# Loads, mask, strided row order and normalisation of the first attention batch

## The chip, the core and the metric

One core of one Trainium2 chip runs the whole program. The metric is device time in microseconds of one execution; the kernel before took 893.43 us (median of 3 runs, 892.42 to 893.95).

## What is computed

Sparse attention, then two MLPs. q, k and v have shape (4 batches, 8 heads, 576 positions, 64).

- Heads 0 to 3 (local): a query sees itself and the 31 positions before it.
- Heads 4 to 7 (strided): a query sees earlier positions with the same remainder modulo 32, itself included; that is 18 positions (j) for each of the 32 residues (r).
- Scores are scaled by 1/8, masked, put through a softmax (sum plus 1e-9) and multiplied by v.
- The result x, 2304 tokens by 512, goes through (x Wa * x Wb) Wo with inner width 1536, then through silu(x Win) Wout2 with inner width 2048. The weights come as float64.

```
scores = where(mask, q @ k.T / 8, -1e9);  attn = softmax(scores);  x = attn @ v
y = ((x @ w_a) * (x @ w_b)) @ w_out
h = y @ w_in2;  out = (h * sigmoid(h)) @ w_out2
```

## The kernel before, in words

**Words.** The float64 weights are cut into pieces of 128 x 512 values. Each arrives as 32-bit words, 512 KB in one of five buffers ("words"), and is converted to float32 on the core. The first six pieces (0 to 5) go a short way: step 0 on GpSimd (L739), step 1 on VectorE (L747), a rebase on ScalarE (L701, tile e), step 2 on VectorE (L752). A buffer is free when its words have been read by these. Then split_w (L774, L775) makes two fp32r halves, with which TensorE multiplies in three passes. Pieces 0 to 4 are a0, b0, a1, b1 (columns of Wa, Wb) and o0 (rows of Wo). Later pieces are converted by sign_w, merge_w and rebase_w inside the blocks, some blocks ahead, and are stored for later token groups.

**First batch.** Attention of batch 0 runs before any block, as a pipeline over nine units: 0 to 4 are local (windows of 128 queries, the last of 64), 5 to 8 are strided (the groups of residues of RES). The loop at L937 runs stages s = -1, 0, 1, ..., and in each stage emits the steps of ORDER = "AXPV0QWS1LGRTBKUON2Y". Each engine works in the order in which its instructions are emitted. For stage s:

- S: scores of unit s on TensorE. Only in the first batch the mask is put into PSUM by a product with the identity (L459), in front of the products (L466).
- L, G: maxima of unit s (L488), and 1e-9 added to the sums of unit s-1 (guard, L523), both VectorE.
- X: exponentials of unit s-1, ScalarE (L500).
- N: reciprocal on VectorE (L527) and product on GpSimd (L538) for unit s-1.
- T, U: transposes (L558) and copies (L567, L572) for unit s-3. V, O: products with v (L607) and stores (L636 ScalarE, L639 VectorE) for unit s-5.
- R: prepare; for strided units GpSimd scales the queries into qs, one instruction for each residue group (L427). PREP puts units 5 and 6 into stage 3, unit 7 into 5, unit 8 into 7.
- Q: transposes of the strided tables on VectorE (L325). P: the local tables.
- 0, 1, B, 2, Y: conversion of piece CONV[s] and split of the one of the stage before. A: half of a first product of blocks 0 to 3 (PART; L782 into acc). K: idle products that keep TensorE warm (L885).
- W: loads that LOADS gives to stage s.

LOADS[-2] is issued before the loop. A capital letter puts the load on ScalarE's queue, the others go on SP's, which issues in order. q, k: local tables; t: strided q, k (qld, kld); m: masks; s: strided v (vs, 16 transfers of 45 or 13.5 KB); w: words; u: next batch's q, k; b: cast of the strided mask. Local v (vl) goes on GpSimd's queue.

**Row order of strided units.** Constant mask rows come as (j, r). The kernel keeps query rows as (r, j), so the mask is loaded in six transfers that permute its rows (L910), and cast into mask_str by GpSimd at stage 3. The columns of the products with v are written through a "p r j" view of PSUM, which makes them (j, r) again for the store.

**Afterwards** come blocks, one for each product with a piece for a token group of 512. Batches 1 to 3 are spread over the blocks by plan_attention: batch 1 transposes its q, k in blocks 0 and 1, and its normalisation, too, is on GpSimd. Within a block, words of the piece eight blocks on are loaded.

Of the kernel before, what the change touches and what calls it, by code (L numbers as in the profile page):

```python
# [9 lines left out]
F32 = mybir.dt.float32  # L10
F32R = mybir.dt.float32r
BF16 = mybir.dt.bfloat16
# [5 lines left out]
ALU = mybir.AluOpType  # L18
AX = mybir.AxisListType

P = 128
STRIDE = 32
HALF = 64
TAKE = 3

RES = [(0, 3, 6), (9, 12, 15), (18, 21, 24), (27, 29)]
# [14 lines left out]
LOADS = {  # L41
    -2: (
        "q0 Q1 i M1 k0 K1 K2 Q2 t8 m7 s2 w0 s2 s1 w2 s2 s1 w1 s1 s1 s1 w4 "
        "w3 s5 u2 u5 u2"
    ),
    3: "b",
    8: "w5 w6",
    10: "w7",
    11: "w11",
    12: "w8 w9",  # L50
    16: "w10",
}
# [8 lines left out]

CONV = {5: 0, 8: 1, 10: 2, 11: 3, 13: 4, 14: 5}
PART = {11: 0, 12: 1, 15: 2, 16: 3}
# [65 lines left out]
def attention_gated_mlp_silu_mlp(  # L129
# [15 lines left out]
    nc = tc.nc  # L145
# [41 lines left out]
    ident_b = cpool.tile([P, P], BF16, name="ident_b")  # L187
    lead.tile([P, 32], F32, name="lead")
    mask_loc = apool.tile([P, 4, HALF], BF16, name="mask_loc", bufs=1)
# [82 lines left out]
    class Batch:  # L272
# [125 lines left out]
        def prepare(self, u):  # L398
# [20 lines left out]
            else:  # L419
                res = RES[i]  # L420
                ng = len(res)
                st = dict(w=JR, segs=2 * ng, slots=ng, n=J * (res[-1] - res[0] + TAKE))
                st["mask"] = mask_str.unsqueeze(1).to_broadcast([P, 2 * ng, JR])
                qh = queries[i % 2]
                if self.first:
                    for g, r0 in enumerate(res):
                        nc.gpsimd.tensor_scalar_mul(  # L427
                            qh[:, :, g, :JR].rearrange("p c (r j) -> p c r j", r=TAKE),
                            qT.rearrange("p c (j r) -> p c r j", r=STRIDE)[:, :, r0:r0 + TAKE],
                            SCALE,  # L430
                        )
# [97 lines left out]
        def normalise(self, u):  # L529
            ty, i = self.units[u]  # L530
            st = self.state[u]
            segs, w, ng = st["segs"], st["w"], st["slots"]
            rs = st["rs"]
            if self.first:
                self.invert(u)
            pr, rs = st["pr"][:, :ng, :, :w], rs.rearrange("p (i g) -> p g i", i=2)
            rs = rs.unsqueeze(3).to_broadcast([P, ng, 2, w])
            nc.gpsimd.tensor_tensor(out=pr, in0=pr, in1=rs, op=ALU.mult)  # L538

# [34 lines left out]
        def values(self, *us):  # L574
# [6 lines left out]
            for u in us:  # L581
                i, st = self.units[u][1], self.state[u]
                pt = st["pt"]
                for g in range(st["slots"]):
                    for k in range(2 if ty == 0 else 1):
                        for hp in range(2):
                            for c in range(2):
# [8 lines left out]
                                else:  # L596
                                    r0 = RES[i][g]
                                    keys = slice(HALF * hp, HALF * hp + JR)
                                    out = banks[hp][rows, :first["cols"]].rearrange("p (j r) -> p r j", j=J)
                                    parts.append((  # L600
                                        out[:, r0 - RES[self.units[us[0]][1]][0]:][:, :TAKE],
                                        vs[keys, firsts.index(r0), c, :],
# [273 lines left out]
    with tc.manual_schedule():  # L876
# [17 lines left out]
        masks[0] = masks[0].rearrange("p (s k) -> p s k", k=HALF)  # L894
        nc.gpsimd.memset(masks[1], 0.0)

        def startup_loads(names):

            for name in names.split():
# [5 lines left out]
                elif name[0] == "m" and n == 1:  # L905
                    feed[0].dma_start(out=masks[0], in_=mask_loc_d)
                elif name[0] == "m":
                    for h in range(0, P, HALF):
                        for r in range(TAKE):
                            feed[0].dma_start(  # L910
                                out=masks[1][h + J * r:h + J * (r + 1)],
                                in_=mask_str_d[h:h + JR].rearrange("(j r) k -> r j k", r=TAKE)[r],
                            )
                elif name[0] == "b":
                    nc.gpsimd.tensor_copy(out=mask_str, in_=masks[1])
                elif name[0] in "qk":
# [580 lines left out]
        p = 0  # L1497
# [130 lines left out]
```

## Time and profile before

| what | value |
|---|---|
| median of 3 runs | 893.43 us (892.42 to 893.95) |
| profiled execution | 891.74 us |
| its span, first to last instruction | 890.0 us |
| mean granted TensorE clock | 0.996 |
| TensorE busy | 876.0 us (98%) |
| VectorE busy | 633.4 us (71%) |
| ScalarE busy | 542.7 us (61%) |
| GpSimd busy | 162.2 us (18%) |
| HBM | 149 GB/s over the span |

The profile is of one execution. Engines: PE is TensorE, PEld its weight loads, DVE VectorE, ACT ScalarE, POOL GpSimd, SP SyncE; SPq is SP's queue issuing transfers. L538 is line 538. Shares over the whole span average a start, in which a chain through all engines decides, with a long rest in which TensorE is hardly ever idle.

### The profile page before, as it was taken

Reading aid. Unit: us, or ns where it says so; the run is one execution under the profiler, and the core shown is the slowest. Engines: PE = TensorE matmul, PEld = TensorE weight load, DVE = VectorE, ACT = ScalarE, POOL = GpSimd, SP = SyncE. Lnnn points to the kernel's source line nnn. Section 1 sums busy time; section 2 is a strip of 40 time slices with the busy share of each in tenths; the row PEclk is TensorE's granted clock in tenths of the full one; section 3 lists DMA queues with packets and bytes.
Section 4 is the critical chain, followed back from the end, with each engine's and each line's share of the span. In section 5 each row is a group of like instructions: output and inputs, shape, how many; then the busy total and the mean of one; then the engine's idle time right before and its main releaser. Section 6 shows DMA issues by size and latency. Waiting matters only on the chain.

```text
span 890.0 us, 16103 instructions
## 1 busy us (share of the span) xinstructions
PE 876.0 (98%) x5859; PEld 728.6 (82%) x5866; DVE 633.4 (71%) x1175; ACT 542.7 (61%) x1296; POOL 162.2 (18%) x232
## 2 busy tenths in 40 slices
PE   8799999999999999999999999999999999999998
PEld 5578788888887788899888888888888888898987
DVE  4687877767667665888776768776777697766664
ACT  4779898676786756675444344755554565455553
POOL 5664564444433110100000000000000000000000
PEclk9899999999999999999999999999999999999999
DMA  9999999798999922664122122321121242311201
GB/s 185 220 252 294 281 282 295 228 288 266 311 301 269 304 82 95 190 190 143 47 72 62 57 71 71 115 75 59 60 72 53 93 162 71 132 59 51 80 1 71
DMA packets 152977, 133.77 MB, mean 150 GB/s; under 512 B 91522, under 2 KB 114690, under 8 KB 152898
## 3 DMA queue, kind: packets, MB, share of 16 engines
q1 hardware_dynamic: 143986, 108.59, 43.4%
q0 software_dynamic: 7424, 23.34, 7.2%
q8 instruction: 46, 0.75, 0.3%
q10 hardware_dynamic: 1488, 0.82, 0.3%
q14 instruction: 33, 0.27, 0.1%
HBM read 110.16 MB, written 22.54 MB: 149 GB/s over the span
## 4 chain that ended last, share of the span: by engine, by line
PE 86%; DVE 5%; ACT 4%; DMA 2%; issue 1%; POOL 1%; SPq 1%; POOLq 0%; ACTq 0%; DVEq 0%
PE ring L782 17%; PE acc L1167 13%; PE ring L1103 12%; PE att L1103 9%; PE ring L1167 7%; PE att L1167 7%; PE acc L1103 7%; PE acc L1538 6%; PE acc L1566 3%; PE att L607 1%; ACT prs L500 1%; PE acc L885 1%; PE att L466 1%; DMA vs<-in_v_dram 1%; DVE w L775 1%
## 5 line engine op out<-in xcount | busy, mean ns | idle before, releaser
L1432 DVE TENSOR_TENSOR w<-raw,w 128x512 fp32r<-128x512 f32 (+1 forms) x164 | 103.2, 641 | 14.8 <-ACT w L1431 14.1
L782 PE MATMUL ring<-x1a,w 128*128 128x256 f32 (+1 forms) x480 | 99.0, 327 | 0.0
L1431 ACT CAST w<-raw 128x512 fp32r<-128x512 f32 (+1 forms) x164 | 93.1, 581 | 7.3 <-ACT w L1431 3.0
L1103 PE MATMUL ring<-L,w 128*128 128x512 f32 x360 | 87.8, 389 | 0.0
L1216 POOL DMA_DIRECT2D out_dram<-o x12 | 6.5, 543 | 407.8 <-DVE o L1215 398.9
L1103 PEld LDWEIGHTS ring<-L,w 128*128 128x128 f32 x360 | 67.6, 188 | 14.0
L1167 PE MATMUL acc<-w,h 128*128 128x512 f32 x288 | 78.5, 391 | 0.0
L782 PEld LDWEIGHTS ring<-x1a,w 128*128 128x128 f32 x480 | 71.5, 190 | 7.7
L775 DVE TENSOR_TENSOR w<-raw,w 128x512 fp32r<-128x512 f32 x80 | 61.6, 777 | 14.2 <-ACT w L774 14.1
L1538 PE MATMUL acc<-h,w 128*128 128x512 f32 x288 | 70.5, 394 | 0.6 <-ACT h L792 0.4
L792 ACT CAST h<-h 128x512 fp32r<-128x512 f32 (+1 forms) x48 | 27.2, 567 | 71.9 <-DVE h L1140 40.5
L1538 PEld LDWEIGHTS acc<-h,w 128*128 128x128 f32 x288 | 53.2, 188 | 12.4 <-ACT h L792 0.6
L1167 PEld LDWEIGHTS acc<-w,h 128*128 128x128 f32 x288 | 53.6, 188 | 9.4 <-DVE h L793 0.4
L727 POOL TENSOR_SCALAR raw<-words 128x512 f16<-128x512 uint8 x56 | 51.8, 926 | 42.5 <-DMA words<-in_moe_w_out_dram 9.8
L782 PE MATMUL ring<-x,w 128*128 128x512 f32 x240 | 58.2, 394 | 0.3 <-DVE w L775 0.3
L1167 PE MATMUL acc<-h,w 128*128 128x256 f32 (+1 forms) x288 | 53.5, 336 | 0.0
L782 PEld LDWEIGHTS ring<-x,w 128*128 128x128 f32 x240 | 44.3, 188 | 10.6 <-DVE w L775 1.6
L1167 PE MATMUL ring<-w,h 128*128 128x512 f32 x192 | 51.9, 391 | 0.0
L774 ACT CAST w<-raw 128x512 fp32r<-128x512 f32 x80 | 49.2, 623 | 1.3 <-DMA raw<-keptp 1.3
L1167 PEld LDWEIGHTS acc<-h,w 128*128 128x128 f32 x288 | 45.2, 190 | 5.7
L793 DVE TENSOR_TENSOR h<-h,h 128x512 fp32r<-128x512 f32 (+1 forms) x48 | 30.9, 643 | 26.4 <-ACT h L792 26.4
L1167 PE MATMUL att<-w,h 128*128 128x512 f32 x192 | 49.3, 391 | 0.0
(263 smaller groups left out, 1908.6 us busy)
## 6 DMA issues: line engine op xcount, KB each, us to landing
raw<-keptp SPq DMA_DIRECT2D x64, 256.0 KB
words<-in_moe_w_out_dram SPq DMA_DIRECT2D x28, 512.0 KB
raw<-kepti SPq DMA_DIRECT2D x48, 256.0 KB
raw<-kepto SPq DMA_DIRECT2D x45, 256.0 KB
words<-in_moe_w_in_dram SPq DMA_DIRECT2D x16, 512.0 KB
raw<-keptb SPq DMA_DIRECT2D x32, 256.0 KB
raw<-kepta SPq DMA_DIRECT2D x31, 256.0 KB
words<-in_moe_w_a_dram SPq DMA_DIRECT2D x12, 512.0 KB
```

The source lines that it names most:

```text
L727: nc.gpsimd.tensor_scalar(out=halves_of(made[c], F16, 1), in0=bytes_of(words[c], 8, 7), scalar1=-TINY, scalar2=127.5 * TINY, op0=ALU.mult, ...
L774: nc.scalar.copy(out=o[:, 0], in_=t)
L775: nc.vector.tensor_tensor(out=o[:, 1], in0=t, in1=o[:, 0].bitcast(F32), op=ALU.subtract)
L782: nc.tensor.matmul(ps[:, :T], lhsT=w[:, wi, c * P:(c + 1) * P], rhs=x[:, xi, c, :T], start=(c == 0 and wi == 0 and xi == 0), stop=(c == CC ...
L792: nc.scalar.copy(out=o[:, 0, :T], in_=t32[:, :T])
L793: nc.vector.tensor_tensor(out=o[:, 1, :T], in0=t32[:, :T], in1=o[:, 0, :T].bitcast(F32), op=ALU.subtract)
L1103: nc.tensor.matmul(self.acc[acc], lhsT=w[:, wi, (2 * part + c) * P:(2 * part + c + 1) * P], rhs=x[:, xi, c], start=(begin and c == 0 and m ...
L1167: nc.tensor.matmul(o, lhsT=lhsT, rhs=rhs, start=(first and wi == 0 and xi == 0), stop=(last and wi == 1))
L1431: nc.scalar.copy(out=o[:, 0, cols], in_=t)
L1432: nc.vector.tensor_tensor(out=o[:, 1, cols], in0=t, in1=o[:, 0, cols].bitcast(F32), op=ALU.subtract)
L1538: nc.tensor.matmul(accs[d], lhsT=w[:, wi, d * P:(d + 1) * P], rhs=h[:, xi], start=(j == 0 and wi == 0 and xi == 0), stop=(j == N1 - 1 and ...
L1566: nc.tensor.matmul(accs[t][:, :DM], lhsT=h[:, xi, t * P:(t + 1) * P], rhs=w[:, wi, :], start=(j == 0 and wi == 0 and xi == 0), stop=(j == ...
```

## The change

- The strided mask is loaded in one transfer, in the order of the constant, and cast at stage 4 into a tile of its own, mask_first. The first batch keeps its strided query rows as (j, r). For the later batches mask_str is filled by six small copies from mask_first (c, stage 16).
- Words 0 to 4 are loaded in front of strided v. The next batch's q, k, three transfers at a time, follow words 6, 7 and 8; word 11 is left to the blocks.
- Pieces 1 and 2 are converted one stage earlier.
- In the first batch the normalisation's product is on VectorE.

```diff
 LOADS = {
-    -2: (
-        "q0 Q1 i M1 k0 K1 K2 Q2 t8 m7 s2 w0 s2 s1 w2 s2 s1 w1 s1 s1 s1 w4 "
-        "w3 s5 u2 u5 u2"
-    ),
-    3: "b",
-    8: "w5 w6",
-    10: "w7",
-    11: "w11",
-    12: "w8 w9",
-    16: "w10",
+    -2: "q0 Q1 i M1 k0 K1 K2 Q2 t8 m7 w0 w1 w2 w3 w4 s8 s8",
+    4: "b",
+    6: "w5",
+    8: "w6 u3",
+    10: "w7 u3",
+    12: "w8 u3",
+    14: "w9",
+    15: "w10",
+    16: "c",
 }
-CONV = {5: 0, 8: 1, 10: 2, 11: 3, 13: 4, 14: 5}
+CONV = {5: 0, 7: 1, 9: 2, 11: 3, 13: 4, 14: 5}
...
+    mask_first = lead.tile([P, 64], BF16, name="lead")[:, :JR]
...
+                rows = mask_first if self.first else mask_str
+                st["mask"] = rows.unsqueeze(1).to_broadcast([P, 2 * ng, JR])
...
-                            qh[:, :, g, :JR].rearrange("p c (r j) -> p c r j", r=TAKE),
-                            qT.rearrange("p c (j r) -> p c r j", r=STRIDE)[:, :, r0:r0 + TAKE],
+                            qh[:, :, g, :JR].rearrange("p c (j r) -> p c j r", r=TAKE),
+                            qT.rearrange("p c (j r) -> p c j r", r=STRIDE)[..., r0:r0 + TAKE],
...
-            nc.gpsimd.tensor_tensor(out=pr, in0=pr, in1=rs, op=ALU.mult)
+            engine = nc.vector if self.first else nc.gpsimd
+            engine.tensor_tensor(out=pr, in0=pr, in1=rs, op=ALU.mult)
...
-                                    out = banks[hp][rows, :first["cols"]].rearrange("p (j r) -> p r j", j=J)
+                                    out = banks[hp][rows, :first["cols"]].rearrange("p (j r) -> p j r", j=J)
+                                    out = out[..., r0 - RES[self.units[us[0]][1]][0]:][..., :TAKE]
...
-                                        out[:, r0 - RES[self.units[us[0]][1]][0]:][:, :TAKE],
+                                        out if self.first else out.rearrange("p j r -> p r j"),
...
-        nc.gpsimd.memset(masks[1], 0.0)
+        nc.gpsimd.memset(mask_str, 0.0)
...
                 elif name[0] == "m":
+                    feed[0].dma_start(out=masks[1], in_=mask_str_d)
+                elif name[0] == "c":
                     for h in range(0, P, HALF):
                         for r in range(TAKE):
                             feed[0].dma_start(
-                                out=masks[1][h + J * r:h + J * (r + 1)],
-                                in_=mask_str_d[h:h + JR].rearrange("(j r) k -> r j k", r=TAKE)[r],
+                                out=mask_str[h + J * r:h + J * (r + 1)],
+                                in_=mask_first[h:h + JR].rearrange("(j r) k -> r j k", r=TAKE)[r],
                             )
                 elif name[0] == "b":
-                    nc.gpsimd.tensor_copy(out=mask_str, in_=masks[1])
+                    nc.gpsimd.tensor_copy(out=mask_first, in_=masks[1])
```

## Rows read from the trace of the kernel before

**Rows 1.** Busy time by stretch: stretch, length, busy time (instructions) per engine, PEclk, DMA share, GB/s
```profile
20.00:22.00 2.00, 1.67 (x50) 1.26 (x50) 1.95 (x6) 0.70 (x4) 1.57 (x4) 1.00 0.36 90
...
25.00:30.00 5.00, 4.18 (x95) 2.91 (x95) 3.61 (x16) 4.15 (x26) 3.46 (x6) 0.61 0.95 214
30.00:35.00 5.00, 4.78 (x87) 2.88 (x90) 2.42 (x10) 4.20 (x26) 3.46 (x5) 0.71 0.77 232
...
130.00:890.00 760.00, 753.95 (x4507) 637.30 (x4497) 541.51 (x973) 444.72 (x993) 83.80 (x118) 1.00 0.44 133
```

**Rows 2.** Timeline of TensorE: start, length, line, operands, count [idle before, releaser]
```profile
21.26 1.48 PE L466 MATMUL acc<-kT,qs 64*64 64x54 f32 x24 [0.25 <-POOL qs L427]
...
27.01 0.32 PE L459 MATMUL att<-mask_str,ident_b 128*128 128x162 bf16 x1 [0.81 <-DVE x L639]
...
36.93 0.57 PE L607 MATMUL acc<-pt,vs 54*64 54x54 f32 x24
...
44.35 8.45 PE L782 MATMUL acc<-x,w 128*128 128x512 f32 x36
...
54.05 0.51 PE L1538 MATMUL acc<-h,w 128*128 128x512 f32 x1 [0.40 <-ACT h L792]
```

**Rows 3.** Waits of TensorE up to 110 us: total us, times, longest
```profile
PE ring L558 <- POOL prs L538: 1.8, 1, 1.8
```

**Rows 4.** Timeline of GpSimd
```profile
20.43 0.23 POOL L915 CAST mask_str<-mask 128x54 bf16<-128x54 f32 x1 [2.60 <-DMA mask<-in_mask_str_dram]
20.63 3.25 POOL L427 TENSOR_SCALAR qs<-qT 128x108 f32<-128x108 f32 x6
23.86 1.17 POOL L538 TENSOR_TENSOR prs<-prs,rs 128x256 f32<-128x256 f32 x2
25.11 0.64 POOL L739 TENSOR_SCALAR x<-words 128x512 int32<-128x512 uint8 x1
...
36.38 0.98 POOL L538 TENSOR_TENSOR prs<-prs,rs 128x324 f32<-128x324 f32 x1 [2.02 <-ACT prs L500]
...
70.90 1.12 POOL L727 TENSOR_SCALAR raw<-words 128x512 f16<-128x512 uint8 x1 [2.73 <-DMA words<-in_moe_w_out_dram]
```

**Rows 5.** Timeline of VectorE
```profile
16.97 0.75 DVE L325 STREAM_TRANSPOSE qT<-qld 128x576 f32<-128x576 f32 x1
...
19.90 1.44 DVE L325 STREAM_TRANSPOSE kT<-kld 128x576 f32<-128x576 f32 x2 [1.32 <-DMA mask<-in_mask_str_dram]
...
25.79 0.46 DVE L747 TENSOR_SCALAR x<-words 128x512 uint8<-128x512 uint8 x1 [3.81 <-POOL x L739]
...
34.38 0.46 DVE L747 TENSOR_SCALAR x<-words 128x512 uint8<-128x512 uint8 x1 [1.69 <-POOL x L739]
...
36.68 0.70 DVE L523 TENSOR_SCALAR su<-su 128x4 f32<-128x4 f32 x1
...
39.74 0.46 DVE L747 TENSOR_SCALAR x<-words 128x512 uint8<-128x512 uint8 x1 [1.19 <-POOL x L739]
...
74.74 0.75 DVE L639 TENSOR_TENSOR x1b<-att,x1a 128x256 fp32r<-128x256 f32 x2
```

**Rows 6.** Timeline of ScalarE
```profile
24.35 0.68 ACT L701 ACTIVATE e<-words 128x512 f32<-128x512 f32 x1 [2.11 <-DMA words<-in_moe_w_a_dram]
...
26.55 0.31 ACT L500 ACTIVATE prs<-acc,nm 128x54 f32<-128x54 f32 x1 [0.85 <-DVE nm L488]
```

**Rows 7.** Timeline of SP's queue: start of an issue, time that it took, count
```profile
13.75 4.01 SPq L910 DMA_DIRECT2D mask<-in_mask_str_dram  x6
...
20.12 0.40 SPq L675 DMA_DIRECT2D words<-in_moe_w_a_dram  x1
...
29.34 4.51 SPq L395 DMA_DIRECT2D vs<-in_v_dram  x5
...
47.79 0.37 SPq L675 DMA_DIRECT2D words<-in_moe_w_b_dram  x1
55.28 0.34 SPq L673 DMA_DIRECT2D words<-in_moe_w_out_dram  x1
```

More of the change, by code (lines that the diff above doesn't have):

```diff
@@ L187, in attention_gated_mlp_silu_mlp @@
     ident_b = cpool.tile([P, P], BF16, name="ident_b")
-    lead.tile([P, 32], F32, name="lead")
+    mask_first = lead.tile([P, 64], BF16, name="lead")[:, :JR]
     mask_loc = apool.tile([P, 4, HALF], BF16, name="mask_loc", bufs=1)
@@ L422, in prepare @@
                 st = dict(w=JR, segs=2 * ng, slots=ng, n=J * (res[-1] - res[0] + TAKE))
-                st["mask"] = mask_str.unsqueeze(1).to_broadcast([P, 2 * ng, JR])
+                rows = mask_first if self.first else mask_str
+                st["mask"] = rows.unsqueeze(1).to_broadcast([P, 2 * ng, JR])
                 qh = queries[i % 2]
```

## The prediction

> **What bounds the kernel now.** I read the busy time by stretch first. From 130 us to the end TensorE is busy 753.95 of 760 us [rows 1]: the reader should see that nothing waits there, so a change of the first batch can only move the moment from which TensorE runs without a break. The timeline of TensorE gives that moment: 36 products in one run at 44.35, the first down product at 54.05 [rows 2]. All that the diff touches has to be priced as a shift of these two rows.
>
> Next I asked who makes TensorE wait before 44.35. The longest wait is 1.8 us, for a normalised prs from GpSimd [rows 3]. GpSimd's timeline says why it was late [rows 4]: it sat idle 2.60 us for the strided mask, cast it at 20.43, then did six query scalings (20.63 to 23.88), and only then the normalisations of units 2 and 3 (23.86 to 25.03) and the first step of word 0 (25.11 to 25.75). VectorE, in order, had the second step of word 0 next and stood idle 3.81 us until 25.79 [rows 5]; the maxima of unit 5 stood behind it, ScalarE's exponentials of unit 5 at 26.55 behind those [rows 6], and TensorE's scores of unit 6 at 27.01 behind VectorE's store of unit 0 [rows 2]. So one knot, between 20 and 27 us, in which GpSimd's order is the cause; TensorE had been through unit 5's scores at 22.74 (21.26 + 1.48) [rows 2]. Later VectorE waits the same way for words 1 and 2: 1.69 us before 34.38 and 1.19 us before 39.74 [rows 5].
>
> **The change part by part.**
>
> *Start of the knot.* The strided tables come first: their kT transposes run at 19.90 to 21.34 [rows 5]. The loads before them on SP are unchanged, so I leave this time. The first-batch mask is one transfer instead of six (4.01 us of SP from 13.75 [rows 7]). I take 2.3 of them for the one, with 0 and 4.01 as bounds: I read the long issue as rings still full of kld, which one transfer meets as well as six. So word 0 is issued at about 16.4 instead of 20.12 [rows 7]. From 20 to 22 us the DMA engines are only 0.36 busy [rows 1]; word 0 fills that and lands by about 21.5 (its reader started at 24.35, after 2.11 us of waiting for it [rows 6]); bounds 19.5 and 24.3.
>
> *GpSimd.* The cast goes behind the six scalings, the nine normalisations leave. The scalings start when qT is turned: 16.97 + 0.75 = 17.7 [rows 5], plus 0.4 for the normalisation that now stands ahead on VectorE: 18.1. Six take 3.25 to 21.35, the cast 0.23 to 21.6, word 0's step 0.64 to 22.25 [rows 4]. The scalings read in another order; bounds 0.25 each (the plain 256 columns of the same engine, 1.17 for two, scaled to 108) and 1.0 (its slowest here, 0.98) [rows 4]; I keep the 0.54 of the row, the same instruction.
>
> *Unit 5 to unit 6.* TensorE: mask product at 21.65, scores to about 22.8 (before 22.74; no gain here). VectorE: word 0's second step 22.3 to 22.8, maxima 22.85 to 23.4 (before, they followed the step that ended at 25.79 + 0.46). ScalarE is done with unit 4 at 22.24 as before (24.35 less the 2.11 idle); e of word 0, a copy and two stores took it from 24.35 to 25.70 (26.55 less 0.85), 1.35, so unit 5's exponentials start at 23.7, 2.8 us before the 26.55 [rows 6]. VectorE's store of unit 0 ends at 24.2, so unit 6's scores start at 24.3 instead of 27.01: **-2.7 us**.
>
> *VectorE normalises.* A normalisation of 256 columns is taken as 0.375, from the store of 128x256 (0.75 for two [rows 5]); 128 columns 0.22, 324 columns 0.45, 216 columns 0.33 in proportion with the same start-up. Bounds for 324 columns 0.3 and 1.0 (GpSimd's slowest, 0.98 [rows 4]), so 1.3 to 4.2 for the five that count below. Units 0 to 3 fall before 22 us, in front of the kT transposes and the 3.81 us hole: nothing, as long as kld lands at 19.9; without this cover 1.5. Units 4 to 8 stand on VectorE where it becomes nearly solid up to 50 us: 0.22 + 3 x 0.45 + 0.33 = **+1.9 us**. VectorE already waits for the same sums of exponentials one step earlier (the guard), so no new wait comes with it; what queues behind each is the merge, the split and the next unit's maxima.
>
> *Words earlier.* With five words ahead of all of strided v, words 1 and 2 are there when their steps come (7 and 9 instead of 8 and 10), and GpSimd has nothing else in front: the holes of 1.69 and 1.19 go: **-2.9 us**. What is late next is VectorE itself, which then runs from 31 to 46 us with two short stops for TensorE's values of units 7 and 8.
>
> *Strided v* now issues behind the words, from about 19 us. Sixteen transfers, at 0.40 when free (as a word's issue) and 0.90 when the rings are full (4.51 for five) [rows 7]: 6.4 to 14.4, I take 9; landed by 30 to 32. Unit 5's values need it at 36.93 - 3.4 = 33.5 [rows 2]. Hidden, with 1.5 us to spare.
>
> *Next batch's q, k and later words.* Three q/k transfers each stand behind words 6, 7 and 8, whose buffers come free at about 29, 34 and 38 us (second steps of words 1 to 3, by the steps above). The last kld is issued at about 40 and lands by 44 with the word ahead of it; VectorE turns it from 46.3. Hidden by some 2 us. SP is relieved: before, word 10 was issued at 55.28, 7.1 us after the issue at 47.79 had ended [rows 7], because its buffer was word 6's; now word 9 and word 10 take the buffers of words 4 and 5 and go at about 43 and 45. The six small copies behind them (step 16) cost SP 0 to 4.0 us (the row of six [rows 7]); I take 4, inside those 7.1 us, for a mask that only the next batch's strided units read.
>
> *Layouts.* Values with the columns in (j r) order: same instructions; 24 of them take 0.57 [rows 2]. I take 0, with a tenth of that either way for each of four units as bounds, 0.2 us.
>
> *Sum.* -2.7 + 1.9 - 2.9 = -3.7: the run of 36 products starts at 40.7 instead of 44.35, the first down product at 50.4. From there the same work follows. It is fed by word loads, and GpSimd already waits 2.73 us for a word at 70.90 [rows 4]; as SP issues from the blocks some 8 us sooner, I take the feed to move along: 0. Against its own execution (span 890.0, 891.74 with what lies around it) that is 888.0; the median of the runs shown, 893.43, lies 1.69 above that execution, so the forecast for the median is **889.7**.
>
> **A rule against it.** While GpSimd's 0.98 us normalisation ran from 36.38, a four-column VectorE instruction took 0.70 at 36.68, twice a store of 256 columns [rows 4, 5]. The Trainium skill (SBUF — State Buffer, SBUF: two separate sides) says that a VectorE instruction with two SBUF inputs shares a port with GpSimd's reads, and that the loser waits for the whole instruction. The moved normalisations are of that kind. By the row, moving them away from GpSimd removes as many such collisions as it brings; by the rule alone five of them could each lose one instruction of GpSimd, which the second rival prices.
>
> **Rivals.**
> 1. *The clock holds.* TensorE's granted clock was 0.61 and 0.71 in 25 to 35 us [rows 1], that is at 1.2 GHz part of the time, after the hole of 1.8 us [rows 3]. My sum keeps the later units' spacing. If the shorter hole leaves the clock at 2.4 GHz, TensorE gains up to 5 x 0.39 + 5 x 0.29 = 3.4 us there, but VectorE, nearly solid, passes on some 1.5: -5.2, 888.2. For it: the hole shrinks from 1.8 us to about 1. Against: short products with gaps remain.
> 2. *VectorE is the new knot.* Five normalisations and the word steps collide with GpSimd's word steps of 0.64 each: +3.2, so -0.5: 892.9. For it: the 0.70 of the row. Against: GpSimd is through with words 1 to 4 by about 30 us.
> 3. *Strided v comes last (the slower side).* If SP stays at the 0.90 or more of the full rings for all sixteen, behind five words that themselves wait, issue ends at 36 and the data lands at 38. Unit 5's values then start 1 us later than the 36.93 of before, and word 5 and the next q, k are behind: +1.1, 894.5. It decides from a landing after 36.9. For it: 0.90 was measured with words in between. Against: that was with as many bytes, begun 3 us later, and still landed in time.
> 4. *The feed doesn't follow.* The first units gain 3.7 but the words of blocks 13 to 18 arrive no sooner than now; GpSimd's 2.73 us grows by what was gained, and TensorE stalls: -1, 892.4.
> 5. *Word 0 does not land sooner* (the change doesn't do what it says): rings full of kld hold it until 24. Then the first 2.7 shrinks to the GpSimd share, about 1; with the rest -2: 891.4.
>
> **How the numbers follow.** Forecast 0.50, rivals 0.16, 0.11, 0.06, 0.08, 0.09. About 0.2% (1.8 us) is what a measurement can tell here, so faster means below 891.6: forecast 0.48 of its 0.50, rival 1 whole, half or more of rival 5, a little of 4: 0.74. Same, up to 895.2: most of 2 and 4, the rest of 5 and half of 3: 0.19. Slower: half of 3 and something unseen: 0.07. The forecast's own range is 888.4 to 891.2. The range reaches down past rival 1 to 887.2 and up to 892.4; outside lie rivals 2 and 3 in the main, and the lower tail, some 0.2.
>
> **What would show it.** Right: GpSimd does its scalings from about 18 us without the 2.60 us idle; VectorE's wait before word 0's second step under 1 us; unit 6's scores at 24.3; no wait of VectorE for GpSimd before the second and third word; the 36 products at 40.7 and the first down product at 50.4; word 10 issued before 47. Wrong: normalisations on VectorE of 0.7 or more, unit 5's values waiting for a vs transfer, the transposes of block 0 waiting for kld, or longer waits for words between 60 and 100 us than before.

## The result and the profile after

The changed kernel took **899.75 us** (median of 5 runs, 896.86 to 901.56) beside 893.15 for the kernel before (5 runs, 891.86 to 893.95): ratio 1.0059 [1.0042, 1.0077]. It is slower by some 6 us where 3.7 less was forecast. Its profiled execution took 897.9 us (span 896.1), 6.2 more than the one before.

The busy time by stretch, kernel after (columns as in [rows 1]):

```profile
30.00:35.00 5.00, 3.75 (x95) 2.59 (x98) 4.93 (x19) 4.28 (x25) 0.10 (x1) 1.00 0.25 57
...
45.00:50.00 5.00, 4.97 (x22) 3.77 (x21) 2.72 (x4) 1.11 (x2) 2.66 (x5) 1.00 1.10 224
50.00:55.00 5.00, 0.00 (x0) 0.00 (x0) 0.07 (x1) 0.00 (x0) 0.00 (x0) 0.82 0.82 180
55.00:60.00 5.00, 2.18 (x65) 1.38 (x65) 2.65 (x4) 1.28 (x3) 1.53 (x2) 0.50 0.68 218
...
130.00:890.00 760.00, 757.59 (x4549) 640.75 (x4549) 544.67 (x977) 449.19 (x1003) 89.47 (x124) 1.00 0.44 134
```

From 130 us on TensorE is as solid as in [rows 1], so the loss lies ahead of it. It is the stretch from 50 to 55: next to nothing is computed, the DMA engines are 0.82 busy. TensorE's timeline of the kernel after shows both sides of the hole (columns as in [rows 2]):

```profile
24.23 0.24 PE L459 MATMUL att<-lead,ident_b 128*128 128x162 bf16 x1
...
34.67 0.57 PE L609 MATMUL acc<-pt,vs 54*64 54x54 f32 x24
...
41.47 8.49 PE L784 MATMUL acc<-x,w 128*128 128x512 f32 x36
57.50 0.42 PE L466 MATMUL att<-kT,qT 64*32 64x64 f32 x4 [7.54 <-DVE kT L324]
...
59.39 5.15 PE L1542 MATMUL acc<-h,w 128*128 128x512 f32 x12
```

Set beside [rows 2], unit 6's mask product stands at 24.23 (before 27.01), unit 5's values at 34.67 (36.93) and the 36 products at 41.47 (44.35). Then TensorE stands 7.54 us, the first down product starts at 59.39 (54.05), and twelve of them take 5.15 us where twelve at the full clock take 2.88 elsewhere, since the granted clock is 0.50 of full, 1.2 GHz, after the hole. VectorE's timeline says what was awaited (columns as in [rows 5]):

```profile
20.26 1.44 DVE L324 STREAM_TRANSPOSE kT<-kld 128x576 f32<-128x576 f32 x2 [0.66 <-DMA kld<-in_k_dram]
...
22.93 0.54 DVE L749 TENSOR_SCALAR x<-words 128x512 uint8<-128x512 uint8 x1
...
28.03 0.50 DVE L539 TENSOR_TENSOR prs<-prs,rs 128x324 f32<-128x324 f32 x1
28.44 1.16 DVE L777 TENSOR_TENSOR w<-x,w 128x512 fp32r<-128x512 f32 x1
29.52 0.90 DVE L749 TENSOR_SCALAR x<-words 128x512 uint8<-128x512 uint8 x1
...
34.99 0.46 DVE L749 TENSOR_SCALAR x<-words 128x512 uint8<-128x512 uint8 x1
...
48.63 1.44 DVE L324 STREAM_TRANSPOSE qT<-qld 128x576 f32<-128x576 f32 x2 [1.29 <-DMA qld<-in_q_dram]
56.67 1.44 DVE L324 STREAM_TRANSPOSE kT<-kld 128x576 f32<-128x576 f32 x2 [6.60 <-DMA kld<-in_k_dram]
```

The three holes of [rows 5] in front of L747 are gone (22.93, 29.52, 34.99 have no wait). In their place VectorE waits 6.60 us for kld, the next batch's strided keys. SP's queue of the kernel after shows why they came late (columns as in [rows 7]):

```profile
14.34 3.22 SPq L910 DMA_DIRECT2D mask<-in_mask_str_dram  x1
17.60 0.44 SPq L677 DMA_DIRECT2D words<-in_moe_w_a_dram  x1
...
20.64 13.56 SPq L394 DMA_DIRECT2D vs<-in_v_dram  x16
...
34.86 0.43 SPq L677 DMA_DIRECT2D words<-in_moe_w_b_dram  x1
35.33 4.17 SPq L310 DMA_DIRECT2D qld<-in_q_dram  x3
39.62 0.57 SPq L675 DMA_DIRECT2D words<-in_moe_w_out_dram  x1
...
40.70 6.31 SPq L310 DMA_DIRECT2D kld<-in_k_dram  x2
47.12 2.25 SPq L677 DMA_DIRECT2D words<-in_moe_w_a_dram  x1
49.41 4.18 SPq L310 DMA_DIRECT2D kld<-in_k_dram  x2
```

The kernel before issued the same eight transfers in one piece:

```profile
33.96 3.26 SPq L311 DMA_DIRECT2D qld<-in_q_dram  x4
37.32 3.13 SPq L311 DMA_DIRECT2D kld<-in_k_dram  x4
```

So the last kld was issued by 53.6 us and not by 40.45. Strided v filled SP's queue to 34.2, and then four kld issues took 10.5 us where they had taken 3.1. GpSimd's timeline of the kernel after:

```profile
18.36 2.98 POOL L427 TENSOR_SCALAR qs<-qT 128x108 f32<-128x108 f32 x6 [4.92 <-DVE nm L488]
...
21.64 0.68 POOL L741 TENSOR_SCALAR x<-words 128x512 int32<-128x512 uint8 x1
...
38.19 0.80 POOL L741 TENSOR_SCALAR x3a<-words 128x512 int32<-128x512 uint8 x1 [8.09 <-DMA words<-in_moe_w_a_dram]
39.05 1.29 POOL L364 DMA_DIRECT2D vl<-in_v_dram  x2
40.33 5.67 POOL L374 DMA_DIRECT2D vl<-in_v_dram  x8
```

Word 5 made GpSimd wait 8.09 us, and behind it, from 39.05 to 46.0, GpSimd issued the next batch's local v on its own queue, just where the last q, k stood. In the kernel before, word 5 was issued behind the keys, at 40.56, so that local v came 7 us later:

```profile
45.26 0.75 POOL L739 TENSOR_SCALAR x3a<-words 128x512 int32<-128x512 uint8 x1 [3.38 <-DMA words<-in_moe_w_a_dram]
46.07 1.27 POOL L365 DMA_DIRECT2D vl<-in_v_dram  x2
```

What GpSimd's queue took from 45 to 50 us is in the DMA view of the kernel after, packets, MB and share of the 16 engines' time (packets overlap, so the shares exceed 100% together):

```profile
q0 software_dynamic: 379, 0.94, 84.8%
q1 hardware_dynamic: 1238, 0.17, 24.6%
```

q0 is GpSimd's queue, q1 SP's and ScalarE's. 379 packets of local v, mostly of 4096 bytes, held the engines; SP's queue, with its 128-byte packets, moved 0.17 MB in 5 us.

### The profile page after: what moved, and what is told of

It is laid out like the page before. It is cut to its first block, busy times and chain, and to the rows that moved or that the text cites. A ratio compares the mean times of both kernels' runs of the same rounds, so it can differ in the third digit from the quotient of the medians.

```text
span 896.1 us, 16095 instructions
## 1 busy us (share of the span) xinstructions
PE 876.6 (98%) x5866; PEld 729.5 (81%) x5866; DVE 639.1 (71%) x1184; ACT 543.0 (61%) x1296; POOL 154.6 (17%) x223
## 4 chain that ended last, share of the span: by engine, by line
PE 90%; ACT 3%; DVE 3%; SPq 2%; issue 1%; DMA 1%; POOL 1%; ACTq 0%; DVEq 0%; POOLq 0%
PE ring L784 20%; PE acc L1171 13%; PE ring L1107 12%; PE att L1107 9%; PE acc L1542 8%; PE ring L1171 7%; PE att L1171 7%; PE acc L1107 7%; PE acc L1570 3%; PE att L609 1%; SPq L310 1%; PE att L466 1%; PE acc L887 1%; ACT prs L500 1%; DMA kld<-in_k_dram 1%
## 5 line engine op out<-in xcount | busy, mean ns | idle before, releaser
L794 ACT CAST h<-h 128x512 fp32r<-128x512 f32 (+1 forms) x48 | 27.2, 567 | 80.4 <-DVE h L1144 40.5
L777 DVE TENSOR_TENSOR w<-raw,w 128x512 fp32r<-128x512 f32 x80 | 62.0, 781 | 13.9 <-ACT w L776 13.8
L1171 PEld LDWEIGHTS acc<-w,h 128*128 128x128 f32 x288 | 53.6, 188 | 9.5 <-DVE h L795 0.4
```

Source lines behind the costliest of these rows:

```text
L777: nc.vector.tensor_tensor(out=o[:, 1], in0=t, in1=o[:, 0].bitcast(F32), op=ALU.subtract)
L794: nc.scalar.copy(out=o[:, 0, :T], in_=t32[:, :T])
L1171: nc.tensor.matmul(o, lhsT=lhsT, rhs=rhs, start=(first and wi == 0 and xi == 0), stop=(last and wi == 1))
```

## The experiments

All are built from the kernel after or before; "before" was run beside each. Times of single rows are of the one profiled execution of each, and words are numbered as in LOADS.

| run | last q, k issued by | key transposes at | TensorE waits for them | first down product | ratio to before |
|---|---|---|---|---|---|
| before | 40.5 | 51.38 | 0 | 54.05 | 1 |
| after | 53.6 | 56.67 | 7.54 | 59.39 | 1.0059 [1.0042, 1.0077] |
| e1_qk_early | 40.6 | 50.43 | 2.51 | 53.11 | 0.9998 [0.9985, 1.0011] |
| e2_vl_on_sp | 47.0 | 50.55 | 0 | 53.23 | 1.0084 [1.0068, 1.0101] |
| e3_before_qk_late | 50.1 | 59.12 | 6.34 | 61.84 | 1.0089 [1.0067, 1.0112] |
| e4_qk_early_pool_norm | 41.5 | 51.91 | 2.38 | 54.59 | 0.9993 [0.9977, 1.0008] |
| e5_interleaved | 37.9 | 49.05 | 1.73 | 51.72 | 0.9972 [0.9956, 0.9989] |
| e7_qk_on_pool | 36.5 | 47.54 | 0 | 50.21 | 0.9978 [0.9960, 0.9996] |
| e8_w5_first | 44.6 | 52.67 | 0 | 55.35 | 1.0010 [0.9995, 1.0024] |
| e9_before_qk_pool | 48.9 | 54.94 | 2.79 | 57.66 | 1.0077 [1.0059, 1.0096] |
| e10_words_on_act | 41.3 | 50.36 | 0 | 53.03 | 1.0015 [1.0004, 1.0027] |
| e11_inter_qk_pool | 40.4 | 50.25 | 0.56 | 52.97 | 0.9981 [0.9967, 0.9995] |
| e12_qk_pool_pool_norm | 46.2 | 54.63 | 5.08 | 57.35 | 1.0050 [1.0031, 1.0070] |
| e13_inter_w5_first | 41.0 | 49.65 | 0 | 52.33 | 0.9972 [0.9959, 0.9985] |

**Is it the late q, k? (e1_qk_early, e3_before_qk_late)** First the kernel after with only their place changed:

```diff
-    -2: "... w0 w1 w2 w3 w4 s8 s8", ... 8: "w6 u3", 10: "w7 u3", 12: "w8 u3",
+    -2: "... w0 w1 w2 w3 w4 s8 s8 u9", ... 8: "w6", 10: "w7", 12: "w8",
```

> The changed kernel with the next batch's q, k loaded as one group behind strided v at the start (none behind words 6 to 8); all else of the change stays. In the changed kernel VectorE stood 6.6 us before kT (until 56.67) and TensorE 7.5 us (until 57.50), and the first down products then ran at 1.2 GHz, 5.15 us instead of 2.88. Both theories (A: q, k are issued too late, behind words whose buffers are not free; B: they are issued in time but starved by local v on GpSimd's queue) expect the wait to go: first down product at about 50.5 to 51.5 and 889 to 891 us, some 3 us under the kernel before. A rival C, that the words and not kld decide, expects a wait of several us for word 5 or 6 in its place, 893 or more.

893.23 us, 0.9998 [0.9985, 1.0011]: what the change lost is back, and the start is sooner than in the kernel after (36 products at 40.21). But nothing is won beside the kernel before: here word 5 stands behind the q, k and takes the wait's place. GpSimd, VectorE and TensorE of this run:

```profile
45.78 0.64 POOL L741 TENSOR_SCALAR x3a<-words 128x512 int32<-128x512 uint8 x1 [15.92 <-DMA words<-in_moe_w_a_dram]
```
```profile
46.46 0.47 DVE L749 TENSOR_SCALAR x3a<-words 128x512 uint8<-128x512 uint8 x1 [3.86 <-POOL x3a L741]
...
50.43 1.39 DVE L324 STREAM_TRANSPOSE kT<-kld 128x576 f32<-128x576 f32 x2
```
```profile
40.21 8.49 PE L784 MATMUL acc<-x,w 128*128 128x512 f32 x36
...
51.22 0.37 PE L466 MATMUL att<-kT,qT 64*32 64x64 f32 x4 [2.51 <-DVE kT L324]
...
53.11 5.50 PE L1542 MATMUL acc<-h,w 128*128 128x512 f32 x12
...
270.92 3.01 PE L784 MATMUL ring<-y,w 128*128 128x512 f32 x12 [2.09 <-DVE g L1534]
```

The key transposes have no DMA wait of their own any more; VectorE is late with them because it waited for word 5. A second loss comes far behind: by ScalarE's casts this run is 0.3 us behind the kernel before up to 264 us and 2.2 behind after that, with a wait of 2.09 us for the tile g in between (last line; 0.21 in the kernel before). So the edit undoes the loss of the start, and the time, 893.23, is that of the rival which gave 893 or more.

The other direction: the kernel before, with only the q, k moved behind words.

```diff
-    -2: "... w4 w3 s5 u2 u5 u2", ... 8: "w5 w6", 10: "w7", 11: "w11",
+    -2: "... w4 w3 s5", ... 8: "w5 w6 u3", 10: "w7 u3", 11: "w11 u3",
```

> The kernel before with only one edit: the next batch's q, k in three groups of three behind words 6, 7 and 11, as late as in the change, instead of at the start. Theory A: kld lands after 52, TensorE waits 3 us or more, 896 to 899 us. Theory B: GpSimd's local v starts when piece 5 is converted, here about 42 us, so the last kld transfers (issued about 44) meet it: a wait of 2 to 6 us, 895 to 899 us, with kld issues of over 2 us each. If neither holds, no wait and 892 to 894 us.

901.34 us, 1.0089 [1.0067, 1.0112]. The start moves by 0.8 us (36 products at 45.16), the rest follows the keys:

```profile
59.96 0.43 PE L466 MATMUL att<-kT,qT 64*32 64x64 f32 x4 [6.34 <-DVE kT L325]
```

That part of the change alone makes the kernel before slower by about as much as the whole change did (1.0089 and 1.0059). Both directions agree: the place of the q, k is the cause of the hole.

**What of it is local v? (e2_vl_on_sp)** The kernel after, with the next batch's local v issued by SP, behind the mask's copies:

```diff
-        feed[0] = nc.gpsimd
         every(batch.load_vl())
-        feed[0] = nc.sync
```

> The changed kernel with the next batch's local v moved from GpSimd's queue to SP's, behind the six mask copies, so that it cannot run beside q, k; the order of q, k is that of the change. Theory B (starved by local v): the kld transfers issue in 0.5 to 1 us instead of up to 5.66, land by 46, kT at 47 to 48.5, no long wait of TensorE, first down product at 50.5 to 51.5; total 889 to 892 us if the later words bear ten transfers in front of them. Theory A (issued too late by order): kld still lands after 53, wait of TensorE over 4 us, 896 or more.

The four kld issues took 2.92 and 2.19 us instead of 6.31 and 4.18, the last was issued by 47.0 instead of 53.6, and VectorE and TensorE waited for no transfer there. Its DMA view from 45 to 50 us:

```profile
q1 hardware_dynamic: 3963, 0.98, 97.6%
```

So local v held the keys back by 6.6 us of issue (53.6 against 47.0), and the order behind the words by the other 6.5 (47.0 against 40.5). That nothing waits for the keys here is owed in part to the start: the 36 products came at 43.52, 2 us later than in the kernel after. The time is no better, 900.48, 1.0084. SP now issued local v from 54.5 to 61.9, so that the word behind it went at 66.25; ScalarE waited 3.74 us for that word, until 70.18, and came late to the copy that TensorE needed next:

```profile
74.61 0.60 PE L609 MATMUL att<-ptl,vl 64*64 64x32 f32 x8 [3.69 <-ACT ptl L568]
```

By ScalarE's casts this run was 0.9 us ahead of the kernel before at 66 us, 3.7 behind at 72 and 8.4 behind from 328 on; what the later steps of that are made of was not tried.

**Normalisation on GpSimd again (e4_qk_early_pool_norm)**, in e1's kernel:

```diff
-            engine = nc.vector if self.first else nc.gpsimd
-            engine.tensor_tensor(out=pr, in0=pr, in1=rs, op=ALU.mult)
+            nc.gpsimd.tensor_tensor(out=pr, in0=pr, in1=rs, op=ALU.mult)
```

> As the first kernel of this group (q, k early), but the first batch's normalisation back on GpSimd. It prices the move of nine normalisations to VectorE. My working before: VectorE +1.9 us on its nearly solid stretch against GpSimd's queue in front of units 2 and 3: with the mask no longer waited for, GpSimd has room, so I expect the same time as the first kernel within 1 us. A rival: GpSimd's order still holds unit 6's scores back by 1 to 2 us, then it is 1 to 2 us slower than the first kernel.

The 36 products come 1.66 us later than in e1:

```profile
41.87 8.46 PE L783 MATMUL acc<-x,w 128*128 128x512 f32 x36
```

VectorE's holes are back too (1.56, 1.35 and 1.37 us of wait for GpSimd's word steps). So in these two profiles the normalisations on VectorE are worth 1.66 us at the start; the times, 893.23 and 894.02, are not told apart by their intervals. Even so the start is 2.5 us sooner than in the kernel before (44.35): the rest of the change has that part.

**Words among strided v, nearly as before (e5_interleaved)**, with q, k behind and the rest of the change kept:

```diff
-    -2: "... w0 w1 w2 w3 w4 s8 s8",
+    -2: "... s2 w0 s2 s1 w1 s2 s1 w2 s1 s1 s1 w3 w4 s5 u9",
```

> The changed kernel with the order of loads undone as a whole: words 0 to 4 between the strided v transfers as in the kernel before, q, k of the next batch behind them at the start; mask, row order, VectorE's normalisation and the earlier steps of words 1 and 2 stay. Theory W (SP's transfers use eight completion semaphores in turn, so strided v issued behind five words waits for each word to land, 13.6 us for 16 transfers, and holds word 5 and q, k): with words in between, the total of SP is about the same, strided v and five words end at 32 to 34 us, word 5 is issued at 39 to 41 and again decides: 892 to 895 us, like the kernel before. If words first were what gains, it is 2 us or more slower than the kernel with q, k early (893.2).

891.14 us, 0.9972 [0.9956, 0.9989], with the earliest 36 products of all, 39.65. Five words in front of strided v are not what makes the start sooner: word 0 is issued at 18.13 here and at 17.60 in the kernel after, words 3 and 4 go out 6 us later. SP issues the same sixteen vs transfers beside them by 31.4 us, the q, k by 37.9. What remains is a VectorE wait of 3.0 us for word 5, a TensorE wait of 1.73, and then the low clock (twelve down products in 4.72).

**q, k from GpSimd's queue (e7_qk_on_pool)**, in the kernel after, behind its last early step on words:

```diff
-    8: "w6 u3", 10: "w7 u3", 12: "w8 u3",
+    8: "w6", 10: "w7", 12: "w8", 13: "g9",      # g: the q, k from nc.gpsimd
```

> The changed kernel with the next batch's q, k on GpSimd's queue, after its step for word 4 (about 30 us, where it stood idle 8 us), instead of on SP behind words 6 to 8. Theory W and the feed: what gives the start's 2.9 us back is SP's one queue, so with eight transfers taken off it words 5 to 10 are issued as their buffers come free (word 5 at 34.3, word 8 before 41), kld lands by 45, no wait of TensorE over 1 us at 50: first down product at 50.5 to 51.5, 889 to 891 us. Rival: small q, k packets on GpSimd's queue are slow to be described or starve beside the words, kT waits again, 895 or more.

891.33 us, 0.9978 [0.9960, 0.9996]. Everything that the prediction had wanted between 40 and 55 us happens in this run's profile: VectorE, then TensorE:

```profile
47.54 1.39 DVE L325 STREAM_TRANSPOSE kT<-kld 128x576 f32<-128x576 f32 x2
```
```profile
40.46 8.50 PE L785 MATMUL acc<-x,w 128*128 128x512 f32 x36
48.89 0.92 PE L467 MATMUL att<-kT,qT 64*32 64x64 f32 x64
50.21 0.49 PE L1543 MATMUL acc<-h,w 128*128 128x512 f32 x1 [0.40 <-ACT h L795]
...
59.40 2.88 PE L1543 MATMUL acc<-h,w 128*128 128x512 f32 x12
```

The two times are 40.46 and 50.21, where 40.7 and 50.4 were forecast. The profiled execution took 888.9, near the 889.7 forecast, but it is among the fastest: the executions run from 887.7 to 895.0 with the median at 891.3.

**Word 5 ahead of the q, k (e8_w5_first)**, in the kernel after:

```diff
-    6: "w5", 8: "w6 u3", 10: "w7 u3", 12: "w8 u3",
+    6: "w5 u9", 8: "w6", 10: "w7", 12: "w8",
```

> The changed kernel with q, k of the next batch as one group right behind word 5 on SP, in front of word 6. Word 5 is issued at 34.3 and lands before 38, kld is issued by 42. If local v on GpSimd's queue (from 39 us, as word 5 is early) starves the rest of q, k, kT comes after 50 and TensorE waits 2 us or more: 893 to 896 us. If not, both waits (word 5, kT) are gone: 889 to 891 us.

894.68 us, 1.0010 [0.9995, 1.0024]. TensorE waits for no key, but the start went wrong: word 0 was issued at 18.48, VectorE waited 2.6 us for its step, TensorE 2.4, and after it six products of a half took 2.87 us at 1.2 GHz where they take 1.64; 36 products at 45.62. So it does not show what word 5's place is worth. It does bear on local v: GpSimd issued it from 41.78, beside the four kld issues, and these took 3.10 us all the same (e13 likewise: local v from 37.99, the kld 3.23 us). Local v's packets flow only some us behind its issue (in the kernel after q0 has 4.0% of the engines' time from 36 to 44 us and 78.0% from 44 to 50), and keys that are through by then are not held.

**Words from ScalarE's queue (e10_words_on_act)**, so that SP has mask, strided v and q, k alone:

```diff
-    -2: "... m7 w0 w1 w2 w3 w4 s8 s8", 4: "b", ... 8: "w6 u3", 10: "w7 u3", 12: "w8 u3",
+    -2: "... m7 s8 s8 u9", 3: "W0 W1", 4: "b W2 W3 W4", ... 8: "w6", 10: "w7", 12: "w8",
```

> The changed kernel with words 0 to 4 issued from ScalarE's queue at stages 3 and 4, and strided v and the next batch's q, k on SP right behind the mask. Theory W: strided v no longer stands behind words on SP's eight semaphores, so its 16 transfers take 6 to 9 us instead of 13.6, q, k are issued by 34 and word 5 at 33 to 35; waits for word 5 and kT go: first down product 50 to 52, 889 to 892 us; ScalarE pays some 2 us of issue at 18 to 22 us. Rival: the DMA engines, not the semaphores, limit strided v; then it takes 12 us or more here too, and the total stays at 893 or above.

The time is 894.66, 1.0015 [1.0004, 1.0027], where 889 to 892 was expected: the rival's side of the expectation came. Strided v still took 13.22 us of SP, which waited for words though these were on another queue:

```profile
SPq L395 <- DMA words<-in_moe_w_a_dram: 4.8, 2, 3.3
SPq L395 <- DMA words<-in_moe_w_b_dram: 4.7, 3, 1.8
```

In the records each transfer of these two queues sets one of eight completion semaphores in turn, and an issue waits for the transfer eight before. (The figures are the wait in all, how often, and the longest.) So a queue of its own for the words does not untie strided v from them. From 18 to 26 us the DMA engines' share was 0.99 to 1.18, and there the engines may have held strided v as well; from 26 to 36 us it was 0.20 to 0.41, which leaves the eight semaphores. The words, issued sooner, also held up the first batch's kld and mask (VectorE waited 3.6 us, GpSimd 3.16 for the mask, TensorE 4.2 for the mask's cast).

**GpSimd's queue alone (e9_before_qk_pool)**: the kernel before with the q, k on it.

```diff
-    -2: "... w3 s5 u2 u5 u2",
+    -2: "... w3 s5", ... 13: "g9",
```

> The kernel before, with only the next batch's q, k moved from SyncE's queue at the start to GpSimd's at stage 13. Tells whether GpSimd's queue by itself gains what the kernel after gained with it (0.9978). Theory: before's q, k were never late, so moving them gains nothing where a chain through all engines sets the time: the 36 products stay at 44.0 to 44.6 us, the first down product at 53.5 to 54.5, and the time is 893 within 1.2 (0.999 to 1.001). Rival Q (the queue is the gain): words 5 and 6 are issued sooner, the first down product comes 2 us or more sooner, and the time is 891 or less. Rival L (issued too late at stage 13, beside local v of the same queue): the key transposes wait, TensorE idles at about 52 us, and the time is 895 or more.

901.02 us, 1.0077 [1.0059, 1.0096]. The start is that of the kernel before (36 products at 44.53, 44.35 there), so taking q, k off SP's queue moves nothing in it. Then comes the late issue that the expectation named as a rival: GpSimd, which normalises in this kernel, came to the q, k at 42.1 us and was through at 48.9, and TensorE waited 2.79 us for the keys. In e7, with normalisations on VectorE, it was through at 36.5. What the queue would give this kernel with the keys in time is not shown.

**The same queue, normalisation on GpSimd (e12_qk_pool_pool_norm)**, to price the move with no late transfer:

> The kernel after with q, k on GpSimd's queue at stage 13 (0.9978 with the normalisation on VectorE), and the first batch's normalisation back on GpSimd. No late transfer hides the difference here. The prediction's term (VectorE's normalisations cost 1.9 us on the path): the 36 products come sooner than the 40.46 of that run, at about 38.6, and the time is 889.5. Rival (GpSimd's products, at 0.61 us and behind its conversions of words, hold the chain back): the 36 products come later, at 41.5 to 42.5, and the time is 892 to 893. Third way: both within 0.5 us of 40.46, the same time within 0.1 per cent.

The first batch's normalisation alone differs from e7. The run cannot price it as meant, since GpSimd again came late to the q, k (39.4 to 46.2), TensorE waited 5.08 us, and the time is 898.15, 1.0050. But it shows the start: the 36 products come at 41.92, 1.46 us later (0.6 of it is a half product that took 2.25 us instead of 1.64 at a lower clock), and VectorE's holes are back, though the words come first as in the kernel after:

```profile
29.77 0.47 DVE L749 TENSOR_SCALAR x<-words 128x512 uint8<-128x512 uint8 x1 [1.36 <-POOL x L741]
...
35.58 0.46 DVE L749 TENSOR_SCALAR x<-words 128x512 uint8<-128x512 uint8 x1 [1.37 <-POOL x L741]
```

**The two best together (e11_inter_qk_pool)**, interleaved words and q, k on GpSimd's queue:

> The kernel after, with words 0 to 4 put between the groups of strided v as in the kernel before, and the next batch's q, k taken off SyncE's queue and issued from GpSimd's at stage 13. Theory (only the q, k and the words behind them cost time; the first-batch edits gain): the 36 products start at 39.6 to 40.3 us (39.65 with the interleaved order, 40.46 with words first), the key transposes wait for no transfer, the first down product comes some 4 us sooner than before (49.5 to 50.5), and the time is 887.5 to 890 us, 0.996 of before or less. Rival C (word 5 takes the wait's place): VectorE and GpSimd wait for word 5 as they did in the interleaved run (3 us near 45 us), the first down product is at 51 to 52, and the time stays near 891. Rival Q (GpSimd's queue is what helps, whatever the start): the same time as with words first and q, k on GpSimd's queue, 891 within 1, though the start is sooner.

891.82, 0.9981 [0.9967, 0.9995]: no better than either. Two things took the start's gain in the profile: one half product fell into a stretch of low clock,

```profile
35.35 2.91 PE L788 MATMUL acc<-x,w 128*128 128x512 f32 x6
```

so the 36 products were at 42.08; and words 5 to 7, free to go at 31.5 to 35 us, ran beside the q, k, whose transposes came at 50.25.

**Interleaved, word 5 ahead of the q, k (e13_inter_w5_first):**

```diff
-    -2: "... w4 s5 u9", ... 6: "w5",
+    -2: "... w4 s5", ... 6: "w5 u9",
```

> The interleaved order of the run that took 0.9972, with word 5 issued between the last strided v and the next batch's q, k (it can go at about 31.4 us, when word 0's buffer has been read) and not behind them (38.0). Theory (that run still lost time because VectorE waited 3.0 us for word 5, which put the key transposes 1.7 us behind TensorE): the wait for word 5 goes, the q, k are all issued by 38.5, the key transposes start at 46 to 47.5, TensorE's scores of block 0 follow the 36 products with no wait, the first down product is at 49.5 to 50, and the time is 888.5 to 890 (0.9945 to 0.996). Rival C' (word 5's 512 KB delay the q, k instead): the key transposes wait for kld, TensorE waits 1 to 3 us for them, and the time is 891 to 893. Rival K (the granted clock): an idle piece of some 2 us on TensorE near 32 us sends the clock to 1.2 GHz for one of the half products (2.9 us in place of 1.64), the 36 products are at 42 or later, and the time is 891 or more whatever the transfers do.

891.21, 0.9972 [0.9959, 0.9985]. The wait for word 5 and TensorE's wait for keys are gone, as expected, but the time is no better than e5's: word 0 was issued at 19.20 in this profile, TensorE waited 2.44 us for the step on it (unit 6 at 26.46), and the 36 products were at 42.61. In the four profiles with VectorE normalising, word 0 issued at 17.6 to 18.1 and no half product at 1.2 GHz they were at 39.65 to 41.47.

## Why the prediction was wrong

**The step that failed** is "Next batch's q, k and later words": "The last kld is issued at about 40 and lands by 44 ... Hidden by some 2 us." Measured: issued by 53.6, turned from 56.67, 7.54 us on TensorE. Three faults in it:

- The words' buffers were taken as what releases words 6 to 8 (29, 34, 38 us). It was SP that was not free: strided v was priced at 9 us, from bounds of 6.4 to 14.4, and took 13.56, near the upper end. 3.7 of that are waits for words (1.7, 1.0, 1.0), through the eight semaphores; the rest was not taken apart. Word 6 went at 34.86, word 7 at 39.62, word 8 at 47.12. Strided v itself was in time, as forecast (unit 5's values at 34.67); its cost fell on what stood behind it, which its own slack of 1.5 us said nothing of.
- The q, k issues were counted as issues of a free ring. With words between them and local v beside them they took 4.17 us for three and 6.31 for two.
- Local v on GpSimd's queue was not in the sum at all. GpSimd issues it behind its step on word 5. In the kernel before that word stood behind the keys, and local v was issued from 46.07 to 53.3, when the keys had all been issued. The change puts word 5 ahead of the keys (34.34), and GpSimd, with no normalisation left to do, stood waiting for it: local v starts at 39.05, ahead of the last keys. In e3, where word 5 is early too (34.06) but GpSimd normalises, it starts at 43.55.

The prediction also took words 9 and 10 for relieved, word 10 "issued before 47": it went at 55.38, behind the keys.

From these terms the shift can be added up again: -2.9 at the 36 products, +7.54 of the hole and +0.6 in the slower scores behind it make 5.2, and the first down product is 5.3 late. The granted clock behind the hole, 1.2 GHz, has no place in the prediction, but it hardly adds to that: twelve products cost 5.15 instead of 2.88 us, yet by ScalarE's casts the shift is still 5.3 at 77 us, well behind the slow stretch, which ends at about 63. It goes on to 6.4 at 83 us, swings between 5.6 and 6.7 up to 103, and is 6.2 at the end (of the profiled executions). e7, with the full clock at its down products, loses about half a microsecond over the same steps (3.8 ahead at 66 us, 3.3 from 328 us on). What these last steps are made of is open.

**The start: a sum nearly right from wrong terms.** 36 products at 41.47, -2.9 where -3.7 was forecast. The knot went as described: scalings at 18.36 (18.1 forecast), the mask's cast done at 21.52 (21.6), word 0's step at 21.64, unit 5's exponentials 23.77 (23.7), unit 6 at 24.23 (24.3). That the mask would be one transfer of 2.3 us: 3.22 here, 1.9 to 4.1 over the runs. But the terms behind it are credited wrongly. "VectorE normalises: +1.9" prices VectorE's side alone: five normalisations do take 0.43 + 3 x 0.50 + 0.38 = 2.3 us of it, yet with them on GpSimd the 36 products come 1.66 and 1.46 us later in two pairs of single profiles (e1 and e4, e7 and e12), so that the move as a whole is a gain there. And the holes of "Words earlier" (-2.9) go by this move, not by the words: with words first and GpSimd normalising they stay at 1.36 and 1.37 (e12). GpSimd's word steps had stood behind its normalisations; "GpSimd has nothing else in front" belonged to the other edit. What is left of the gain, some 2.5 us with the normalisations undone (e4: 41.87 against 44.35), lies with the mask, the row order and the earlier conversions, and none of these was undone alone; that the words come first does not make it (e5).

As to the second rival, the five normalisations took 0.38 to 0.50 us each in the kernel after, with no stretch to be seen; in e1 one of 256 columns took 0.80 instead of 0.43 (21.82), beside GpSimd's step on word 0 (21.68 to 22.34). Beside GpSimd's later steps on words (27.34 to 30.1) L777 took 1.16 us instead of 0.68 and L749 0.90 instead of 0.46 in the kernel after. That is 0.9 us in all, not the rival's 3.2. The Trainium skill (SBUF — State Buffer, SBUF: two separate sides) says that a VectorE instruction with two SBUF inputs and a GpSimd one that reads SBUF share a pair of ports, and that the one that starts first has it for the whole instruction. L777 and e1's normalisation, which have two inputs, roughly agree with that; the five of the kernel after show no such wait.

**The feed.** "I take the feed to move along: 0" does not hold in the runs. e7 was 3.8 us ahead of the kernel before at 66 us and 3.3 from 328 us on; e1 was 0.9 ahead at 49 and 2.3 behind at the end (with 2.51 us of wait for the keys and 1.9 more for g among it); e2 lost 9.3, in part since local v was late.

**The rivals.** The slower side was put on strided v landing too late for unit 5 (0.06). It names the right queue and nearly the right issue time (36 there, 34.2 measured), with the wrong victim. "The transposes of block 0 waiting for kld" stood among the signs and had no price; the kernel before had 51.38 - 40.5 = 11 us between its last kld issue and the transposes, and the change spent all of it. The reading there that VectorE turns kld from 46.3 takes qld's row, 50.02, for kld's, 51.38; by that the forecast would be 47.7, which changes nothing in the sum. Rival 1's condition came true without its gain: the granted clock was 1.00 from 30 to 35 us (0.71 before), and the 36 products moved by 2.9, not by 5.2. Rival 3 named the next q, k as the thing behind strided v, but its price was that of unit 5.

**What stays open.** Four versions (e5, e7, e11, e13) stand at 0.9972 to 0.9981 of the kernel before, though their profiles have the first down product anywhere from 50.21 to 52.97. When word 0 is issued (17.60 and 18.48 with words first, in the kernel after and e8; 17.75 and 19.20 interleaved, in e11 and e13) and where a stretch of 1.2 GHz falls differ between profiles of one order by as much as these versions differ. There is a later loss as well, which the experiments did not touch: between some 258 and 328 us most versions fall back by another 0.8 to 3.1 us against the kernel before, through a wait for g near 270 (2.09 in e1, 1.94 in e2, 1.45 in e11), a stop of 0.9 at 296.6 (e5) or a stretch of 1.2 GHz near 300 (e4, e10, e13). Of the four best profiles only e7's has none of it, and it has the shortest span, 887.1 against 889.7 to 889.9. Single profiles do not tell the four apart, and a kernel that has all their gains at once was not found.

## What to carry to other kernels

When a load moves to a later place in a queue, price every issue between its old place and its new one, and set the end of that against the moment when its data is read; the slack of the transfer in front does not cover the one behind. Ask what other queue will be sending at that time: few large packets there can hold up many small ones here. And test each edit's share by undoing it alone: here a forecast start came out nearly right while the credit for it went in part to the wrong edit.

## What the runs showed of the hardware

- From 45 to 50 us in the kernel after, GpSimd's queue held 84.8% of the DMA engines' time with 379 packets; SP's 128-byte packets got through at 0.17 MB in 5 us, and one kld issue took 5.66 us. With local v elsewhere SP's queue had 97.6% and moved 0.98 MB, keys and words.
- SP's and ScalarE's transfers share eight completion semaphores in this program, so an issue can wait for a word of another queue: up to 3.3 us for one of 512 KB in e10.
- After an idle piece of 7.5 us TensorE was granted 1.2 GHz from about 53 to 63 us (worked out from the 0.82, 0.50 and 0.66 of the stretches); after one of 2.5 us as well (twelve products in 5.50). Six products of a half took 2.87 to 2.91 us at 1.2 GHz and 1.64 at 2.4.
